# Rope attention and a squared-ramp MLP on one core: the same steps issued in another order, and some copies on the other engine

## The chip, the cores and the metric

The kernel runs on one core of a Trainium2 chip. The metric is device time in microseconds (us) of one execution; a kernel's time is the median of several executions. Engines are named as the profile names them: PE (TensorE matmul), PEld (its weight loads), DVE (VectorE), ACT (ScalarE), POOL (GpSimd) and SP (SyncE, which here issues every DMA).

## What is computed

Four batches, eight heads, 576 tokens, head size 64; then an MLP over the 2304 tokens (512 to 2048 to 512). The reference, cut to what matters:

```python
q_rot, k_rot = (rotate(q), rotate(k))              # rotary positions, halves x1, x2
scores = scale * np.matmul(q_rot, k_rot.transpose(0, 1, 3, 2))
scores = scores - np.max(scores, axis=-1, keepdims=True)
attn = np.exp(scores)
attn = attn / (np.sum(attn, axis=-1, keepdims=True) + 1e-09)
x = heads_together(np.matmul(attn, v))              # 2304 x 512
h = x @ w_in
g = np.where(h >= 1, h, np.where(h <= -1, 0.0, (h + 1) ** 2 / 4))
return g @ w_out
```

## The kernel before

**Precision.** Most operands are held as two f16 parts, a high part and a rest, and a product is three f16 matmuls (high by high, high by rest, rest by high). Splitting a tensor `x` with a factor `f` is one copy `high = f16(x*f)` and one `rest = x*f - high`. The copy may run on ACT (L311, L707) or on DVE (L313, L710). The ramp of the MLP has a square that runs on DVE (L696, one instruction) or on ACT (L698 and L699, two). The function `pick` reads the string `ON_VECTOR`, one digit per such choice in the order in which the plan is built: 1 is DVE, 0 is ACT.

**Stages.** Batch 0 works in f32: k and q are rotated on DVE by two products with the tables (L284, L285), summed on PE with an identity matrix (L302, L303, two matmuls into a PSUM region `psX`) and copied out by ACT (L306), or summed on DVE (L292). A score group (L555 for batch 0, L557 later) fills two PSUM tiles, `psS0` and `psS1`, one per head, columns 0 to 575; `psX` is the columns from 576 on of the same two tiles. Softmax of a group, `softmax_item`: DVE takes each head's maximum (L527), ACT the exponential with its sum (L529, L532), DVE a reciprocal (L534), then each head's high copy and rest (L538). A DMA transpose (L240) turns the result into `pT`, and PE multiplies by v (L605); `x_out` (L616, L619) writes x. An MLP block of 256 tokens is 8 steps: L684 into `psH`, ACT's ramp L701, the square, L704, the high copy, L712, then L721 into `psO`; at the end ACT copies out (L732) and SP stores.

**Weights.** The 16 weight chunks (8 of w_in, 8 of w_out, 1 MB each) come as 64-bit numbers (L236). DVE packs each in three instructions (L486, L488, L490), ACT makes the high copy (L311), PE forms the rest (L423, L424), ACT writes it (L427). Of the first chunk of each matrix a scale is measured first: two squares on ACT (L245), a sum over partitions on PE (L252), five or six tiny DVE instructions (L257, L259, L262, L269, L502). v's scale is measured the same way: three squares of `rv` and `rvL` (L245) and one L252.

**What sets the order.** `Plan.add` collects 2140 steps, each for one engine, with the tiles that it reads and writes. Nothing is scheduled at run time: `Plan.order` walks the table `ORDER`, each number being the place of the next step in the list of those still left, and the steps are issued in that one sequence. Each engine then works through its own steps in that order, and the waits between engines follow from which step stands first in the whole sequence. Two steps that touch the same PSUM bank wait for each other even if their columns differ, the later one in the sequence for the earlier one. The number `F32_SCORES` is a cost noted with batch 0's score steps; the issued sequence does not read it.

Of the kernel before, what the change touches and what calls it, by code (L numbers as in the profile page):

```python
# [21 lines left out]


ORDER = """
# [54 lines left out]
"""  # L79


PE_TILES = 16
PE_SUMS = 4
PE_V = 1
F32_SCORES = 1060.0
ON_VECTOR = (
    "00000000000000000000000000000000000000000000000000000000000000000000011100001000000000000000000000100100"
    "10101000011001010000110101000001101101000100000110000111000110100001011101000000010001111101101111010110"
    "10100110100010110000011000101000011001000011001001110111100001011111110010110101011001010010100111000101"
    "1000011001111111"  # L90
)


class Plan:


    def __init__(self):
        self.steps = []
        self.writer = {}
        self.readers = {}  # L100
        self.group = "init"
        self.part = ""
        self.free = []
# [36 lines left out]
def kernel(  # L140
# [187 lines left out]
    def qFkeys(hf, j):  # L328
        return [("qT", hf, 2 * (j % 2) + e, j // 2) for e in range(2)]
# [213 lines left out]
    def scores(at, b, t, j):  # L543
# [16 lines left out]
        if b == 0:  # L560
            plan.add("pe", F32_SCORES, at, mm, r=qFkeys(hf, j) + [("kT", ks, j, x) for x in range(2)],
                     w=[("psS", 0), ("psS", 1)], mode="rows")
# [312 lines left out]
```

## Time and profile before

| | before |
|---|---|
| median of 3 runs | 636.51 us (634.36 to 637.54) |
| the profiled execution's own time | 638.57 us |
| its span, first to last instruction | 636.8 us |
| PE busy | 591.4 us (93%) |
| DVE busy | 510.9 us (80%) |
| ACT busy | 417.3 us (66%) |
| mean granted TensorE clock | 0.96 |

Busy time is the time in which an engine has an instruction under way. The share is an average over the span: what an engine's idle time costs is read in the stretch where it falls. [...] The profiled execution is one run, 2.1 us above the median of the three.

### The profile page before, as it was taken

How to read it: one execution, taken by the hardware profiler on the slowest of the kernel's cores; microseconds unless marked ns; L12 is line 12 of the kernel's file. 1: busy time of each engine (PE TensorE's matmuls, PEld its weight loads, DVE VectorE, ACT ScalarE, POOL GpSimd, SP SyncE). 2: the span in 40 equal slices, each digit the busy share in tenths (PEclk: the TensorE clock that was granted, in tenths of full speed). 3: DMA queues.
4: the chain of work that ended last, by engine and by line, in shares of the span. 5: the costliest groups of instructions: out<-in, count | busy, mean ns of one | idle time of the engine just before them, and what ended most of it. 6: DMA issues, size and time to landing. Idle time of an engine off the chain costs nothing.

```text
span 636.8 us, 12019 instructions
## 1 busy us (share of the span) xinstructions
PE 591.4 (93%) x4770; PEld 379.4 (60%) x4770; DVE 510.9 (80%) x823; ACT 417.3 (66%) x843; POOL 0.7 (0%) x6
## 2 busy tenths in 40 slices
PE   4668878998999999999999999999999999999997
PEld 3343434655566667565666676666666666667674
DVE  5777597998999999999988999898989778854333
ACT  1666686988998878668787566655855765624321
POOL 0000000000000000000000000000000000000000
PEclk9775599999999999999999999999999999999999
DMA  8768799867485966677776643555764654550000
GB/s 308 275 200 205 228 219 294 211 168 180 123 217 143 220 137 137 153 165 151 146 157 154 159 108 66 98 90 104 131 125 91 127 95 97 79 87 34 1 34 18
DMA packets 182568, 91.29 MB, mean 143 GB/s; under 512 B 170608, under 2 KB 171888, under 8 KB 180464
## 3 DMA queue, kind: packets, MB, share of 16 engines
q1 hardware_dynamic: 182512, 90.52, 61.2%
q8 instruction: 37, 0.61, 0.4%
q14 instruction: 19, 0.16, 0.1%
HBM read 40.96 MB, written 4.72 MB: 72 GB/s over the span
## 4 chain that ended last, share of the span: by engine, by line
PE 52%; DVE 16%; ACT 7%; DMA 6%; issue 2%; SPq 0%; ACTq 0%; DVEq 0%
PE psH L684 20%; PE psO L721 20%; PE psV L605 4%; PE psS L557 4%; DMA pT<-phl 4%; DVE sca L527 3%; DVE phl L538 3%; ACT p L529 2%; PE psS L423 2%; DVE r L704 2%; DVE g L712 1%; DVE phl L313 1%; ACT phl L311 1%; PE psS L555 1%; DMA dup<-in_km_dram 1%
## 5 line engine op out<-in xcount | busy, mean ns | idle before, releaser
L684 PE MATMUL psH<-xT,w 128*128 128x256 f16 (+1 forms) x1920 | 205.1, 262 | 0.9 <-ACT a L701 0.9
L721 PE MATMUL psO<-w,g 128*128 128x512 f16 x864 | 201.4, 379 | 1.4 <-ACT o L732 0.8
L684 PEld LDWEIGHTS <-w 128*128 128x128 f16 x1920 | 170.5, 98 | 34.5 <-issue 3.2
L529 ACT ACTIVATE p<-psS,sca 128x576 f32<-128x576 f32 x144 | 105.6, 736 | 72.0 <-DVE sca L527 45.8
L721 PEld LDWEIGHTS <-g 128*128 128x128 f16 x864 | 82.0, 98 | 87.7 <-issue 3.5
L527 DVE TENSOR_REDUCE sca<-psS 128x1 f32<-128x576 f32 x144 | 106.0, 751 | 20.4 <-ACT w L427 4.7
L538 DVE SCALAR_TENSOR_TENSOR phl<-p,sca,phl 128x576 f16<-128x576 f32 x144 | 116.1, 812 | 6.9 <-ACT phl L311 6.2
L311 ACT ACTIVATE phl<-p,sca 128x576 f16<-128x576 f32 x98 | 73.8, 767 | 23.5 <-DVE sca L534 16.9
L701 ACT ACTIVATE a<-psH 128x512 f32<-128x512 f32 x72 | 42.5, 591 | 43.4 <-PE psH L684 35.4
L704 DVE SCALAR_TENSOR_TENSOR r<-a,r 128x512 f32<-128x512 f32 x72 | 49.4, 686 | 22.1 <-ACT r L699 21.4
L712 DVE SCALAR_TENSOR_TENSOR g<-r,g 128x512 f16<-128x512 f32 x72 | 49.5, 687 | 11.4 <-ACT g L707 9.3
L557 PE MATMUL psS<-kT,qT 64*128 64x64 f16 (+1 forms) x576 | 44.8, 284 | 2.6 <-ACT p L529 2.6
L605 PE MATMUL psV<-pT,vS 128*64 128x256 f16 (+1 forms) x512 | 43.3, 293 | 0.4 <-DVE sca L262 0.4
L557 PEld LDWEIGHTS <-qT 64*128 64x128 f16 x576 | 22.7, 94 | 32.7 <-issue 16.2
L427 ACT ACTIVATE w<-psS,sca 128x341 f16<-128x341 f32 (+1 forms) x48 | 25.4, 539 | 17.0 <-PE psS L555 8.3
L707 ACT ACTIVATE g<-r 128x512 f16<-128x512 f32 x40 | 24.9, 623 | 17.0 <-DVE r L704 7.1
L698 ACT ACTIVATE r<-a 128x512 f32<-128x512 f32 x46 | 28.8, 625 | 6.8 <-DVE g L712 5.6
L605 PEld LDWEIGHTS <-vS 128*64 128x64 f16 x512 | 27.1, 111 | 8.2 <-issue 4.9
L555 PE MATMUL psS<-kT,qT 64*128 64x512 f32 (+1 forms) x128 | 26.8, 510 | 4.0 <-ACT p L529 3.5
L699 ACT ACTIVATE r<-r 128x512 f32<-128x512 f32 x46 | 29.0, 630 | 1.5
L423 PE MATMUL psS<-xT,kT 128*128 128x341 f32 (+1 forms) x48 | 22.5, 558 | 7.8 <-ACT w L427 5.2
L423 PE MATMUL psS<-o,kT 128*128 128x341 f32 (+1 forms) x48 | 22.7, 561 | 6.4 <-DVE sca L527 3.2
(95 smaller groups left out, 539.6 us busy)
## 6 DMA issues: line engine op xcount, KB each, us to landing
w<-in_w_in_dram SPq DMA_DIRECT2D x7, 1024.0 KB, 5.5
w<-in_w_out_dram SPq DMA_DIRECT2D x6, 1024.0 KB, 6.7
rv<-in_vm_dram SPq DMA_DIRECT2D x8, 512.0 KB, 4.6
out_dram<-o SPq DMA_DIRECT2D x16, 256.0 KB, 2.4
rk<-in_km_dram SPq DMA_DIRECT2D x6, 576.0 KB, 5.1
dup<-in_km_dram SPq DMA_DIRECT2D x6, 576.0 KB, 4.6
dup<-in_qb_dram SPq DMA_DIRECT2D x4, 640.0 KB, 4.8
rq<-in_qb_dram SPq DMA_DIRECT2D x4, 640.0 KB, 6.2
```

Of the source, the lines that this page charges most:

```text
L311: plan.add("act", act_cost(n), at, lambda: nc.scalar.activation(out=hi, in_=x, func=AF.Copy, scale=f), r=r, w=w)
L423: nc.tensor.matmul(out=bank, lhsT=idn, rhs=y[:, cut], start=True, stop=False)
L527: plan.add("dve", dve_cost(S, psum=True), at, lambda m=m, src=src: nc.vector.tensor_reduce(out=m, in_=src, op=ALU.max, axis=AX.X, negate=T ...
L529: plan.add("act", act_cost(S, psum=True, ptrs=2), at, lambda a=a, e=e, m=m, src=src: nc.scalar.activation(out=p32[e], in_=src, func=AF.Exp ...
L538: plan.add("dve", dve_cost(S, ptrs=1), at, lambda a=a, e=e, hi=hi, lo=lo: nc.vector.scalar_tensor_tensor(out=lo, in0=p32[e], scalar=rr[:, ...
L557: nc.tensor.matmul(out=psS[a][:, lo:hi], lhsT=qT[hf][d, l, j, c:c + 128], rhs=kT[ks][d, j, m, lo:hi], start=z == 0, stop=z == 2)
L605: nc.tensor.matmul(out=outs[a], lhsT=st, rhs=moving(a, blk), start=z == 0, stop=z == len(seq) - 1)
L684: nc.tensor.matmul(out=psH[:, n * i:n * i + n], lhsT=wi[ft // 2][:, wl, kk, 128 * (ft % 2):128 * (ft % 2) + 128], rhs=xfn(xl, kk), start=z ...
L701: plan.add("act", act_cost(512, psum=True, ptrs=0), at, lambda one=one: nc.scalar.activation(out=a, in_=psH, func=AF.Relu, scale=2.0 ** -7 ...
L704: plan.add("dve", dve_cost(512), at, lambda one=one: nc.vector.scalar_tensor_tensor(out=r, in0=a, scalar=one, in1=r, op0=ALU.max, op1=ALU. ...
L712: plan.add("dve", dve_cost(512), at, lambda g=g, one=one: nc.vector.scalar_tensor_tensor(out=g[:, 1], in0=r, scalar=-one, in1=g[:, 0], op0 ...
L721: nc.tensor.matmul(out=psO[pos[tt]], lhsT=g[:, gl, n * i + 128 * tt:n * i + 128 * tt + 128], rhs=wo[ft // 2][:, wl, ft % 2, :], start=ft = ...
```

## The change

The table `ORDER` and the string `ON_VECTOR` are replaced, and `F32_SCORES` is another number. The steps are the same 2140, with the same tiles, and every buffer is the same. Of 328 choices 97 name DVE where 110 did: of the high copies more go from DVE to ACT than the other way, of the MLP's squares 19 go to DVE and 16 to ACT. Almost every step stays within some ten places of where it was on its engine.

```diff
 ORDER = """
-2 1 0 0 6 6 24 10 10 0 35 42 0 15 4 0 30 3 61 17 1 10 0 3 30 3 1 73 0 9 27 0 13 19 246 242 5 25 17 2 243 241 0
+3 1 0 0 49 13 6 19 6 1 22 28 0 8 0 38 13 14 23 3 7 25 1 56 15 0 12 1 31 3 70 15 1 0 28 5 22 25 22 0 235 11 238 14
...
-F32_SCORES = 1060.0
+F32_SCORES = 1132.0
...
-    "1000011001111111"
+    "1110100011000000"
```

**Place one, DVE's first ten rows after its constants.** The products with the rotary tables; `w` holds the second, rolled copy of k and q for batch 0, `rk` and `rq_85` the first. Before:

```order
L284 TENSOR_TENSOR rk<-rk,rt 128x576
L284 TENSOR_TENSOR w<-w,rt 128x576
L284 TENSOR_TENSOR rq_85<-rq_85,rt 128x256
L284 TENSOR_TENSOR w<-w,rt 128x256
L284 TENSOR_TENSOR rk<-rk,rt 128x576 x2
L284 TENSOR_TENSOR w<-w,rt 128x576
L284 TENSOR_TENSOR w<-w,rt 128x256
L284 TENSOR_TENSOR w<-w,rt 128x576
L284 TENSOR_TENSOR w<-w,rt 128x256
L284 TENSOR_TENSOR rk<-rk,rt 128x576
L527 TENSOR_REDUCE sca<-psS_93 128x1
```

Now:

```order
L284 TENSOR_TENSOR w<-w,rt 128x576
L284 TENSOR_TENSOR rk<-rk,rt 128x576
L284 TENSOR_TENSOR w<-w,rt 128x256
L284 TENSOR_TENSOR rq_85<-rq_85,rt 128x256
L284 TENSOR_TENSOR w<-w,rt 128x576 x2
L284 TENSOR_TENSOR w<-w,rt 128x256
L284 TENSOR_TENSOR rk<-rk,rt 128x576
L284 TENSOR_TENSOR rq_85<-rq_85,rt 128x256 x3
L284 TENSOR_TENSOR w<-w,rt 128x256 x2
L284 TENSOR_TENSOR rk<-rk,rt 128x576
L527 TENSOR_REDUCE sca<-psS_93 128x1
```

The last product that the first score group needs, the `w` 128x256 of the first head pair, was DVE's fourth instruction and is the seventh; the first maximum (L527) stands behind 14 products where it stood behind 11. SP's loads moved with them: the load for that product was the fifth and is the eighth, behind three more (128x256, 128x576, 128x256), and the load for the second of the two `w` 128x576 in front of it is the ninth.

**Place two, DVE and PE around the third score group** (L555; its two maxima are the two L527 here). `dup_88` and `rq_86` are the rest of batch 0's q, `o` the packed second weight chunk. DVE before:

```order
L534 RECIPROCAL sca<-sca 128x2
L527 TENSOR_REDUCE sca<-psS_93 128x1
L538 SCALAR_TENSOR_TENSOR phl_72<-p_1_70,sca,phl_72 128x576
L284 TENSOR_TENSOR rq_85<-rq_85,rt 128x256
L538 SCALAR_TENSOR_TENSOR phl_73<-p_2_71,sca,phl_73 128x576
L486 TENSOR_SCALAR o<-w 128x1024
L284 TENSOR_TENSOR w<-w,rt 128x256
L488 SCALAR_TENSOR_TENSOR o<-w,o 128x1024
L284 TENSOR_TENSOR rq_85<-rq_85,rt 128x256
L527 TENSOR_REDUCE sca<-psS_92 128x1
```

DVE now:

```order
L534 RECIPROCAL sca<-sca 128x2
L285 SCALAR_TENSOR_TENSOR dup_88<-dup_88,rt 128x1280
L527 TENSOR_REDUCE sca<-psS_93 128x1
L527 TENSOR_REDUCE sca<-psS_92 128x1
L538 SCALAR_TENSOR_TENSOR phl_73<-p_2_71,sca,phl_73 128x576
L490 SCALAR_TENSOR_TENSOR o<-w,o 128x1024
L538 SCALAR_TENSOR_TENSOR phl_73<-p_0_69,sca,phl_73 128x576
```

PE before:

```order
L555 MATMUL psS_92<-kT_62,qT_64 128x64
L555 MATMUL psS_93<-kT_62,qT_64 128x64
L302 MATMUL psS_93<-rk,kT_63 128x288
L303 MATMUL psS_93<-w,kT_63 128x288
L302 MATMUL psS_93<-rk,kT_63 128x288
L303 MATMUL psS_93<-w,kT_63 128x288
L302 MATMUL psS_92<-rq_85,kT_63 128x256
L303 MATMUL psS_92<-w,kT_63 128x256
```

PE now:

```order
L555 MATMUL psS_92<-kT_62,qT_64 128x64
L555 MATMUL psS_93<-kT_62,qT_64 128x64
L302 MATMUL psS_92<-rq_85,kT_63 128x256
L303 MATMUL psS_92<-w,kT_63 128x256
L302 MATMUL psS_93<-rk,kT_63 128x288
L303 MATMUL psS_93<-w,kT_63 128x288
```

The two maxima stand next to each other, where seven instructions stood between them; the sum of the third q pair stands in the whole sequence ahead of the maximum of `psS_92`, where it stood behind it. The second rest of `phl_73`, which the second DMA transpose waits for, was DVE's 50th step and is its 36th.

**Place three, ACT from the first high copies to the first weight squares.** `dup_87<-rv` are the squares of v. Before:

```order
L311 ACTIVATE phl_72<-p_0_69,sca 128x576
L306 ACTIVATE kT_62<-psS_93 128x288
L311 ACTIVATE phl_72<-p_1_70,sca 128x576
L306 ACTIVATE kT_62<-psS_92 128x288
L529 ACTIVATE p_2_71,sca<-psS_92,sca 128x576
L306 ACTIVATE qT_64<-psS_93 128x256
L529 ACTIVATE p_0_69,sca<-psS_93,sca 128x576
L532 ACTIVATE sca<-sca 128x2
L245 ACTIVATE r,sca<-xT_77 128x512 x2
```

Now:

```order
L311 ACTIVATE phl_72<-p_0_69,sca 128x576
L245 ACTIVATE dup_87,sca<-rv 128x1024 x2
L306 ACTIVATE qT_64<-psS_93 128x256
L529 ACTIVATE p_2_71,sca<-psS_92,sca 128x576
L306 ACTIVATE kT_62<-psS_92 128x288
L306 ACTIVATE kT_62<-psS_93 128x288
L529 ACTIVATE p_0_69,sca<-psS_93,sca 128x576
L532 ACTIVATE sca<-sca 128x2
L245 ACTIVATE r,sca<-xT_77 128x512
```

The two squares of v, each waiting for its half of `rv`, stand ahead of the copy of the second q pair and of the second group's exponentials; they stood some ten instructions behind.

## Rows read from the trace of the kernel before

**Rows 1.** Windows: us, then PE, PEld, DVE, ACT, POOL busy, PEclk, DMA share, GB/s

```profile
0.00:60.00 60.00, 37.71 (x113) 21.77 (x113) 39.48 (x75) 31.38 (x65) 0.70 (x6) 0.78 0.77 251
60.00:120.00 60.00, 50.56 (x290) 27.74 (x290) 48.54 (x66) 42.74 (x84) 0.00 (x0) 0.82 0.91 237
120.00:180.00 60.00, 56.49 (x356) 33.63 (x358) 53.06 (x77) 54.24 (x108) 0.00 (x0) 1.00 0.63 161
240.00:300.00 60.00, 57.77 (x527) 37.71 (x526) 56.86 (x92) 46.70 (x96) 0.00 (x0) 1.00 0.71 148
540.00:600.00 60.00, 60.00 (x454) 40.01 (x453) 32.26 (x54) 25.98 (x50) 0.00 (x0) 1.00 0.30 54
```

**Rows 2.** Timeline to the first maxima: start, us, engine, line, what [idle before <-releaser]

```profile
9.13 0.43 DVE L284 TENSOR_TENSOR w<-w,rt 128x256 f32<-128x256 f32 x1 [0.67 <-DMA w<-in_qa_dram]
...
11.21 1.30 PE L555 MATMUL psS<-kT,qT 64*128 64x512 f32 x8 [0.47 <-ACT qT L306]
...
12.60 1.43 DVE L284 TENSOR_TENSOR w<-w,rt 128x256 f32<-128x256 f32 x3 [0.35 <-DMA w<-in_qa_dram]
...
14.61 1.42 DVE L527 TENSOR_REDUCE sca<-psS 128x1 f32<-128x576 f32 x2
```

**Rows 3.** Timeline, third score group to the weight scale's sum

```profile
25.38 1.85 PE L555 MATMUL psS<-kT,qT 64*128 64x512 f32 x8
...
28.44 0.76 DVE L527 TENSOR_REDUCE sca<-psS 128x1 f32<-128x576 f32 x1 [2.92 <-PE psS L303]
...
31.81 1.05 ACT L245 ACTIVATE dup<-rv 128x1024 f32<-128x1024 f32 x1
...
33.31 0.75 DVE L527 TENSOR_REDUCE sca<-psS 128x1 f32<-128x576 f32 x1
...
34.12 1.22 PE L302 MATMUL psS<-rq,kT 128*128 128x256 f32 x2 [3.19 <-DVE sca L527]
...
39.61 0.43 PE L252 MATMUL psS<-sca 128*128 128x3 f32 x2
...
42.05 0.23 DVE L257 TENSOR_REDUCE sca<-psS 128x1 f32<-128x3 f32 x2 [4.19 <-PE psS L555]
```

**Rows 4.** Timeline, the second DMA transpose and what it waits for

```profile
46.57 0.81 DVE L538 SCALAR_TENSOR_TENSOR phl<-p,sca,phl 128x576 f16<-128x576 f32 x1
...
47.45 2.70 SPq L240 DMA_TRANSPOSE pT<-phl  x1
```

**Rows 5.** Windows, narrow ones, columns as in rows 1

```profile
42.00:44.00 2.00, 0.84 (x2) 0.30 (x2) 1.95 (x9) 0.78 (x1) 0.00 (x0) 1.00 0.04 11
44.00:46.00 2.00, 0.30 (x1) 0.10 (x1) 1.81 (x5) 1.34 (x2) 0.00 (x0) 1.00 0.01 4
60.00:80.00 20.00, 17.35 (x63) 8.52 (x63) 12.44 (x17) 10.79 (x22) 0.00 (x0) 0.56 0.81 215
```

**Rows 6.** Groups by line: xcount | busy us, mean ns of one | idle before

```profile
L311 ACT ACTIVATE phl<-p,sca 128x576 f16<-128x576 f32 x98 | 73.8, 767 | 23.5 <-DVE sca L534 16.9 <-DMA pT<-phl 2.9 <-DVE r L704 1.5
L699 ACT ACTIVATE r<-r 128x512 f32<-128x512 f32 x46 | 29.0, 630 | 1.5
L698 ACT ACTIVATE r<-a 128x512 f32<-128x512 f32 x46 | 28.8, 625 | 6.8 <-DVE g L712 5.6 <-DVE sca L534 0.7
L707 ACT ACTIVATE g<-r 128x512 f16<-128x512 f32 x40 | 24.9, 623 | 17.0 <-DVE r L704 7.1 <-PE psO L721 5.1 <-PE psH L684 4.4
L313 DVE TENSOR_SCALAR phl<-p,sca 128x576 f16<-128x576 f32 x46 | 23.7, 516 | 2.8 <-DMA pT<-phl 2.3
L696 DVE SCALAR_TENSOR_TENSOR r<-a 128x512 f32<-128x512 f32 x26 | 17.8, 685 | 12.6 <-ACT a L701 12.2
L710 DVE TENSOR_SCALAR g<-r 128x512 f16<-128x512 f32 x32 | 13.6, 424 | 4.7 <-PE psO L721 3.2
```

**Rows 7.** Timeline, the end

```profile
625.43 6.64 PE L721 MATMUL psO<-w,g 128*128 128x512 f16 x30
...
628.36 0.69 DVE L712 SCALAR_TENSOR_TENSOR g<-r,g 128x512 f16<-128x512 f32 x1
```

More of the change, by code (lines that the diff above doesn't have):

```diff
@@ L84 @@
 PE_V = 1
-F32_SCORES = 1060.0
+F32_SCORES = 1132.0
 ON_VECTOR = (
-    "00000000000000000000000000000000000000000000000000000000000000000000011100001000000000000000000000100100"
-    "10101000011001010000110101000001101101000100000110000111000110100001011101000000010001111101101111010110"
-    "10100110100010110000011000101000011001000011001001110111100001011111110010110101011001010010100111000101"
-    "1000011001111111"
+    "00000000000000000000000000000000000000000000010000010000000000000000000000010000000000000010000000000000"
+    "01100000001001100011010000000011010000010000100001100011001010001000110001011010101011010000011011000100"
+    "00001101100111010001001100100111011100100010110111011001001111101000101000000001110100011011011010110011"
+    "1110100011000000"
 )
```

106 rows, old and new, of the table ORDER are left out of this document.

## The prediction

> **What bounds the kernel now.** I read first the windows of 60 us. PE stands idle 22.3 us of the first 60, 9.4 of the next 60, 3.5 from 120 to 180, 2.2 from 240 to 300 and none from 540 on [rows 1]; its whole idle time is 45.4 us (636.8 less 591.4), so 31.7 of it, 70%, falls before 120 us. [...] The reader is to see two kernels in one: a start in which PE, DVE, ACT and DMA wait for each other in turn, and then a long stretch in which PE is full. PE's work is the same in both kernels, step by step. A new order can gain only where PE waits, so I read the start closely, in the timeline.
>
> From 120 to 300 us three engines are nearly full together (DVE 53.1 and 56.9 of 60, ACT 54.2 and 46.7) [rows 1]. A lead won in the start is therefore kept there if the work behind it is the same, and little is won anew.
>
> **The change part by part.** Working against the profiled execution (span 636.8, own time 638.57, which is 2.1 above the median of 636.51).
>
> *The start becomes later.* The last product for the first score group ran at 9.13, as soon as its load, the fifth, had landed; at 12.60 DVE waited for the tenth load [rows 2]. Between them five loads of 1,280 KB landed in 3.47 us: 369 KB/us. Now that product's load is the eighth, 544 KB later, so it lands at 9.13 + 1.5 = 10.6. On DVE it stands behind a 128x576 product whose load, 288 KB more, lands at 11.4; that one takes about 0.75 (the size of one maximum, L527 [rows 3]), the product itself 0.43 [rows 2], so it ends at 12.6 where it ended at 9.56. The first scores start 1.65 after it [rows 2]: 14.25 for 11.21, 3.0 later. DVE then has seven products left (five of 0.45, two of 0.75, together 3.7) ahead of the first maximum, which so starts at 16.3 for 14.61: part of the delay is already paid back, because before these products stood later.
>
> *The third scores.* They started at 25.38 [rows 3]. Now ACT has v's two squares in front, and the second waits for the twenty-first load. Up to it 6,816 KB are fetched, 5,408 more than at 9.13, which at 369 KB/us is 14.7 us: 23.8. A square takes 1.05 [rows 3], and then five instructions (three copies, two exponentials) of 0.4 to 0.75 come before the third scores, about 2.7 us: 27.6, or 2.2 later. PE's sums stand between them; a score group there took 1.85 where another took 1.30 [rows 2, 3], so up to 1.8 more can come from the slow clock. Bounds +2.2 and +4.0, taken in the middle: **+3.1**.
>
> *From the third scores to the weight scale's sum* (L555 at 25.38 to L252 at 39.61, 14.2 us [rows 3]). DVE took the first maximum at 28.44 and the second only at 33.31, since seven instructions stood between, and the sum of the third q pair, which needs its PSUM bank, waited 3.19 us for it [rows 3]. Now the two maxima are neighbours: the second follows 0.76 after the first instead of 4.87, 4.1 sooner, and the q sum stands ahead of it in the sequence and waits for neither. At least the 3.2 of PE's wait goes; if it and the 4.1 counted in series, 7.3. They overlap in part, so I take the middle: **-5.3**. What is late next is ACT, which has the two weight squares, v's third and the exponentials there in a row.
>
> The q sum writes columns from 576 on and the maximum reads those up to 575, and still it waited [rows 3]. [...]
>
> *The scale's first reduction.* L257 ran at 42.05, 2.0 after its matmul at 39.61 had ended, released by a score group (L555) that stood between in the sequence [rows 3]. Now L257 stands ahead of that group. The group takes 1.30 [rows 2]: **-1.3**; the bounds are 0 and 2.0.
>
> So the weight scale, on which all sixteen chunks hang, is ready some 3.5 us earlier.
>
> *SP.* The second transpose was issued at 47.45, when the second rest (46.57, 0.81 long) was done [rows 4]. SP stood before it, and the DMA engines were idle from 42 to 46 (share 0.04 and 0.01 [rows 5]). That rest moves up 14 places on DVE, ahead of the scale's tiny instructions, so the transpose and the loads behind it start some 8 us sooner; a load of k (576 KB) that stood at the fifty-first place is pulled ahead into that time as well. It is worth nothing if the loads were not late, and at most the 4 us of idle DMA; 60 to 120 is the stretch with DMA share 0.91 [rows 1], so something: **-0.8**.
>
> *Choices of engine.* 71 go from DVE to ACT and 58 back. A softmax high copy takes 0.767 on ACT and 0.516 on DVE, one of the MLP 0.623 and 0.424, a square 1.26 in two on ACT and 0.685 on DVE [rows 6]. Net, DVE loses 13 instructions, some 6 us; up to 300 us, where DVE is fullest, 17 go to ACT and 9 come, about 4 us. Hidden by PE after 300 us, so nothing there; before it, between -4 (all on the path) and +2 (ACT, 54.2 of 60 in one window, is late instead). It is nearest to the hidden case, since PE idles only some 8 us in that stretch: **-0.7**.
>
> *The end.* In the last step square and high copy both go to ACT: 1.26 - 0.685 + 0.623 - 0.424, so 0.77 longer. The last rest ended at 629.05; the last twelve of 30 matmuls, at 0.22 each, began at 629.3 [rows 7]. The new order puts one more group of three (0.65) in front. The cover is 0.25 + 0.65 = 0.9: nothing, and 0.77 at most if it is gone. All other moves are of a few places within full stretches: 0. The new `F32_SCORES` is read by no instruction: 0.
>
> Sum: 3.1 - 5.3 - 1.3 - 0.8 - 0.7 = **-5.0**, so 633.6 for the profiled execution and **631.5** beside the median.
>
> **The rivals.**
>
> *The late start is not made up (slower).* For it: 3 us at the first scores are certain by the loads, and ACT stands behind v's squares, waiting for a load that was no one's limit before. If the sums behind the third scores then wait for ACT instead of for the maximum, the gain of 5.3 is not there and the larger lag of 4.0 stays: 636.5 + 4.0 = 640.5. It decides where the weight scale's sum (L252) starts later than 39.61. Against it: PE's longest wait in that part named DVE [rows 3], and its cause is gone from the order.
>
> *The lead is lost before the MLP (no change).* From 60 to 120 us the DMA share is 0.91 [rows 1]. If the loads set when the first MLP step starts, a lead at 42 us ends there: 636, with what the choices of engine give, 635.5. Against it: the same loads start earlier too.
>
> [...]
>
> That the order does not act as it says is no rival of its own: only a table sets it.
>
> **How the numbers follow.** My forecast, 631.5, has 0.42 (its own range 628.5 to 633.3), the clock 0.12, the lost lead 0.28, the late start 0.18. 0.5%, about what a measurement of this kernel can tell from no change, is 3.2 us: faster means below 633.3, slower above 639.7. So faster 0.54, same 0.28, slower 0.18. The range takes in the clock's 626.5 with 2 us for its unknown size and reaches to the late start's 640.5: 624.5 to 640.5.
>
> **What would show it.** First scores near 14.3 and third scores near 28.5 in the timeline; then the two maxima of that group back to back, the wait of L302 for L527 gone, and L252 near 37.5, L257 right behind it. The second transpose should be issued before 40, and the DMA share from 42 to 46 should not be near 0. PE's first MLP step should start 3 to 5 us earlier, with the idle time of PE from 120 on as before. If L252 starts after 39.6, the forecast is wrong at the third scores; if it starts early and the first MLP step doesn't, it is wrong in DMA; if PE's idle time from 120 to 300 has grown, the choices of engine are to blame.

## The result, and the profile after

| | before | after |
|---|---|---|
| median, runs of the two beside each other | 636.18 us (634.36 to 637.54, 4 runs) | 617.05 us (613.99 to 618.41, 4 runs) |
| the profiled execution's own time | 638.57 us | 617.46 us |
| its span | 636.8 us | 615.7 us |
| PE busy | 591.4 us | 579.5 us |
| DVE busy, ACT busy | 510.9, 417.3 us | 507.0, 422.9 us |
| mean granted TensorE clock | 0.96 | 0.98 |

The ratio is 0.969 (95% interval 0.965 to 0.974): 19.1 us faster. The forecast was 631.5, the range 624.5 to 640.5. The direction was right; the gain is almost four times the forecast, and the time lies below the range.

The granted clock is the profile's, as a share of TensorE's full clock. In the kernel before it is 1.00 from 27 to 33 us, for one, and 0.50 from 48 to 77; "full" and "low" or "half" below stand for readings like these two.

The windows of 60 us after, as in [rows 1] (us, then PE, PEld, DVE, ACT and POOL busy, granted clock, DMA share, GB/s):

```profile
0.00:60.00 60.00, 40.41 (x133) 23.74 (x135) 45.68 (x83) 35.14 (x76) 0.71 (x6) 0.86 0.96 292
60.00:120.00 60.00, 52.59 (x363) 32.08 (x360) 56.51 (x75) 51.58 (x103) 0.00 (x0) 0.97 1.04 249
120.00:180.00 60.00, 60.00 (x449) 36.75 (x448) 59.66 (x92) 57.57 (x114) 0.00 (x0) 1.00 0.76 183
180.00:240.00 60.00, 59.34 (x552) 39.55 (x550) 57.71 (x91) 55.09 (x113) 0.00 (x0) 1.00 0.84 177
240.00:300.00 60.00, 59.79 (x529) 38.51 (x528) 56.87 (x92) 43.47 (x90) 0.00 (x0) 1.00 0.63 139
300.00:360.00 60.00, 57.09 (x555) 39.67 (x553) 50.96 (x86) 40.49 (x80) 0.00 (x0) 0.97 0.59 128
540.00:600.00 60.00, 60.00 (x499) 41.35 (x498) 22.33 (x34) 19.29 (x33) 0.00 (x0) 1.00 0.09 25
```

From 60 to 120 the clock is 0.97 where it was 0.82, and DVE does 56.5 us of work where it did 48.5 [rows 1]. From 120 to 180 PE stands still no more: 60.00, where it was 56.49 [rows 1]. One stretch is worse than before, 300 to 360: PE is busy for 57.09 us, where it was for 59.70 in the same window of before.

Where the 21 us between the two profiled executions arise is read from the start of the same step in both timelines:

| step | before | after | lead |
|---|---|---|---|
| first scores (L555) | 11.21 | 13.78 | -2.6 |
| third scores (L555) | 25.38 | 28.55 | -3.2 |
| weight scale's sum (L252) | 39.61 | 40.43 | -0.8 |
| its first reduction (L257) | 42.05 | 40.75 | +1.3 |
| fifth score group (L555) | 50.54 | 47.55 | +3.0 |
| first MLP step (L684) | 111.16 | 96.51 | +14.7 |
| second MLP block (L684) | 195.51 | 175.53 | +20.0 |
| span | 636.8 | 615.7 | +21.1 |

(The expectation of e6 below counts that score group, at 50.5 us before, as the fourth.) At 48 us the lead is 3.0, near the 3.5 that the forecast had for the weight scale. Then come 11.7 more before the first MLP step and 5.3 up to the second block. For all that the forecast had 0.8 (SP), 0.7 (choices of engine) and nothing for the other moves. Here is the stretch with most of it, 20 to 100 us, first before, then after (windows of 20 us, columns as above):

```profile
20.00:40.00 20.00, 14.43 (x38) 9.16 (x38) 14.86 (x19) 12.20 (x32) 0.00 (x0) 0.67 0.85 268
40.00:60.00 20.00, 13.50 (x40) 6.63 (x39) 13.78 (x33) 13.81 (x24) 0.00 (x0) 0.67 0.57 158
80.00:100.00 20.00, 15.03 (x75) 7.37 (x74) 18.08 (x25) 16.38 (x30) 0.00 (x0) 0.91 0.99 246
```

```profile
20.00:40.00 20.00, 16.30 (x38) 10.20 (x37) 14.63 (x17) 12.58 (x32) 0.00 (x0) 0.58 0.89 266
40.00:60.00 20.00, 13.37 (x63) 6.94 (x63) 19.16 (x40) 18.05 (x35) 0.00 (x0) 0.99 1.06 293
60.00:80.00 20.00, 14.95 (x99) 8.05 (x95) 17.99 (x25) 15.57 (x30) 0.00 (x0) 1.00 1.09 257
80.00:100.00 20.00, 17.64 (x134) 10.74 (x133) 18.87 (x26) 16.80 (x34) 0.00 (x0) 0.91 1.10 262
```

Three things go together from 40 to 80: the clock is 0.99 and 1.00 where it was 0.67 and 0.56 [rows 5], DVE and ACT work more (DVE 37.2 of the 40 us where it worked 26.2, ACT 33.6 where it worked 24.6), and the DMA share is 1.06 and 1.09 where it was 0.57 and 0.81. One trace can't tell which of them leads.

### The profile page after: what moved, and what is told of

It reads as the page before. It is cut to its first block, busy times and chain, and to the rows that moved or that the text cites. A ratio compares the mean times of both kernels' runs of the same rounds, so it can differ in the third digit from the quotient of the medians.

```text
span 615.7 us, 11999 instructions
## 1 busy us (share of the span) xinstructions
PE 579.5 (94%) x4770; PEld 375.3 (61%) x4770; DVE 507.0 (82%) x810; ACT 422.9 (69%) x853; POOL 0.7 (0%) x6
## 4 chain that ended last, share of the span: by engine, by line
PE 60%; DVE 19%; DMA 10%; ACT 7%; issue 4%; SPq 0%; DVEq 0%; ACTq 0%
PE psO L721 20%; PE psH L684 19%; PE psV L605 6%; DVE sca L527 4%; PE psS L557 4%; PE psS L423 3%; DVE phl L538 3%; DMA pT<-phl 3%; PE psS L555 2%; DMA vM<-vS 2%; ACT p L529 2%; DMA w<-in_w_out_dram 2%; DVE g L712 2%; DMA rk<-in_km_dram 2%; DVE r L704 2%
## 5 line engine op out<-in xcount | busy, mean ns | idle before, releaser
L684 PE MATMUL psH<-xT,w 128*128 128x256 f16 (+1 forms) x1920 | 204.9, 262 | 0.0
L684 PEld LDWEIGHTS <-w 128*128 128x128 f16 x1920 | 170.9, 98 | 34.1 <-issue 2.6
L529 ACT ACTIVATE p<-psS,sca 128x576 f32<-128x576 f32 x144 | 105.7, 737 | 56.4 <-DVE sca L527 42.1
L538 DVE SCALAR_TENSOR_TENSOR phl<-p,sca,phl 128x576 f16<-128x576 f32 x144 | 115.2, 812 | 3.8 <-ACT phl L311 3.2
L527 DVE TENSOR_REDUCE sca<-psS 128x1 f32<-128x576 f32 x144 | 106.2, 751 | 10.7 <-PE psS L557 6.9
L701 ACT ACTIVATE a<-psH 128x512 f32<-128x512 f32 x72 | 42.5, 590 | 52.0 <-PE psH L684 46.0
L605 PE MATMUL psV<-pT,vS 128*64 128x256 f16 (+1 forms) x512 | 43.5, 293 | 0.9 <-DMA pT<-phl 0.9
L557 PE MATMUL psS<-kT,qT 64*128 64x64 f16 (+1 forms) x576 | 43.8, 284 | 0.2
L707 ACT ACTIVATE g<-r 128x512 f16<-128x512 f32 x54 | 33.6, 623 | 13.9 <-DVE r L704 12.6
L557 PEld LDWEIGHTS <-qT 64*128 64x128 f16 x576 | 21.5, 94 | 29.5 <-issue 12.2
L696 DVE SCALAR_TENSOR_TENSOR r<-a 128x512 f32<-128x512 f32 x29 | 20.0, 688 | 20.9 <-ACT a L701 20.3
L605 PEld LDWEIGHTS <-vS 128*64 128x64 f16 x512 | 27.0, 112 | 9.5 <-issue 5.4
L698 ACT ACTIVATE r<-a 128x512 f32<-128x512 f32 x43 | 27.0, 627 | 8.0 <-DVE g L712 7.1
L605 PE MATMUL psV<-pT,vM 128*64 128x256 f16 (+1 forms) x320 | 26.2, 293 | 5.5 <-DMA vM<-vS 5.1
L529 ACT ACTIVATION_READ_ACCUMULATOR p<-psS,sca 128x1 f32 x144 | 28.3, 197 | 0.0
L699 ACT ACTIVATE r<-r 128x512 f32<-128x512 f32 x43 | 27.1, 630 | 1.4
```

Of the source, the lines that this page charges most:

```text
L527: plan.add("dve", dve_cost(S, psum=True), at, lambda m=m, src=src: nc.vector.tensor_reduce(out=m, in_=src, op=ALU.max, axis=AX.X, negate=T ...
L529: plan.add("act", act_cost(S, psum=True, ptrs=2), at, lambda a=a, e=e, m=m, src=src: nc.scalar.activation(out=p32[e], in_=src, func=AF.Exp ...
L538: plan.add("dve", dve_cost(S, ptrs=1), at, lambda a=a, e=e, hi=hi, lo=lo: nc.vector.scalar_tensor_tensor(out=lo, in0=p32[e], scalar=rr[:, ...
L557: nc.tensor.matmul(out=psS[a][:, lo:hi], lhsT=qT[hf][d, l, j, c:c + 128], rhs=kT[ks][d, j, m, lo:hi], start=z == 0, stop=z == 2)
L605: nc.tensor.matmul(out=outs[a], lhsT=st, rhs=moving(a, blk), start=z == 0, stop=z == len(seq) - 1)
L684: nc.tensor.matmul(out=psH[:, n * i:n * i + n], lhsT=wi[ft // 2][:, wl, kk, 128 * (ft % 2):128 * (ft % 2) + 128], rhs=xfn(xl, kk), start=z ...
```

## The experiments

**One change or two: the choices alone, the order alone.**

e1_choices, on the kernel before (the last line of the string; the others are replaced too):

```diff
-    "1000011001111111"
+    "1110100011000000"
```


> The order of before, with the engine choices of the change alone. If the new choices are what keeps PE full from 120 to 240 us (theory of the choices), this gains some 9 us, to about 627. If the order does all of it (theory of the order), it stays within 3 us of 636.

e2_order, on the changed kernel (likewise):

```diff
-    "1110100011000000"
+    "1000011001111111"
```


> The order of the change, with the engine choices of before. Theory of the order: 617, within 3. Theory of the choices: PE idles again from 120 to 240 us, and the time is near 626.

Both theories fell. The choices alone gave 650.41 (ratio 1.020, 1.014 to 1.025), 12.9 slower than the 637.47 beside them; the order alone 636.52 (0.999, 0.997 to 1.001), no change; the two together 19 faster. With the order before, the new choices cost 13 us; with the new order they save 19. So what the choices are worth depends on the order.

Both mismatched kernels lose in the same place, behind the first 200 us. The choices alone start the first MLP step at 110.5 and the second block at 194.8, as before; the order alone starts them at 94.9 and 175.7, as the changed kernel. That fits the table of choices: laid over the changed kernel's trace, none of the 129 choices that differ belongs to an instruction that runs before 145 us, and only 9 to one before 200. The start is a matter of the order alone; behind it PE waits. From 200 to 545 us PE stands idle for 4.9 us in the kernel before and 4.4 in the changed one, but for 13.6 with the choices alone and 18.1 with the order alone. The first three rows of PE's waits from 200 us on, first of the choices alone (200 to 545), then of the order alone (200 to 560, its lines one higher) and of the changed kernel (200 to 545); the columns are what PE waited with, for whom, us in total, times, the longest:

```profile
PE psS L557 <- ACT p L529: 6.2, 10, 1.1
PE psH L684 <- ACT a L701: 2.6, 5, 0.8
PE psS L583 <- ACT p L529: 2.1, 2, 1.5
```

```profile
PE psS L558 <- ACT p L530: 6.4, 10, 1.5
PE psV L606 <- DMA vM<-vS: 2.6, 2, 2.2
PE psH L685 <- ACT a L702: 2.4, 6, 0.6
```

```profile
PE psV L605 <- DMA vM<-vS: 2.9, 2, 2.4
PE psV L605 <- DMA pT<-phl: 0.9, 2, 0.7
PE psV L605 <- DMA vM<-vM: 0.4, 1, 0.4
```

In the changed kernel no row of that stretch names ACT, and in the kernel before L557 waits for ACT 5 times, 2.6 us in all. With the choices of the other order ACT's exponentials (L529) and ramps (L701) come late, in pieces of about half a microsecond. Here is the longest of these waits in e1. ACT was itself idle and waited for the second maximum (L527), and ahead of that maximum DVE had a high copy (L313 at 416.42) that ran on ACT before:

```profile
416.42 0.51 DVE L313 TENSOR_SCALAR phl<-p,sca 128x576 f16<-128x576 f32 x1
417.57 0.75 DVE L527 TENSOR_REDUCE sca<-psS 128x1 f32<-128x576 f32 x1
418.36 0.74 ACT L529 ACTIVATE p<-psS,sca 128x576 f32<-128x576 f32 x1 [0.99 <-DVE sca L527]
419.24 0.93 PE L583 MATMUL psS<-kT,qT 64*64 64x512 f16 x23 [1.45 <-ACT p L529]
```

So a moved copy can stand in the way on DVE, and not only in ACT's own queue. How much of the loss comes from such copies, and from which, was not tried.

**Where the order gains: four pieces of it.** e3_start50 takes the change's order for its first 153 steps and the order before for the rest; e4_start100 does so for 333 steps, to the first MLP step; both keep the choices before. e5_rest and e6_rest50 are the complements: the kernel before for 338 or 147 steps, then the changed order, with the changed choices. As first and last lines of the tables, e3 (and e4, which differs further in) and e5 (e6 has the same end, its lines broken elsewhere) against the kernel before:

```diff
-2 1 0 0 6 6 24 10 10 0 35 42 0 15 4 0 30 3 61 17 1 10 0 3 30 3 1 73 0 9 27 0 13 19 246 242 5 25 17 2 243 241 0
+3 1 0 0 49 13 6 19 6 1 22 28 0 8 0 38 13 14 23 3 7 25 1 56 15 0 12 1 31 3 70 15 1 0 28 5 22 25 22 0 235 11 238
```

```diff
-0 5 0 4 0 3 0 2 0 1 0 0 0 0 0 0 1 0
+10 0 0 8 8 15 15 0 7 13 0 6 2 0 4 8 0 0 6 0 5 0 11 4 0 3 8 3 7 7 0 6 0 5 0 0 3 0 2 0 1 0 0 0 0 0 0 0 0
```

> The first 153 steps of the change's order (to the fifth score group, about 48 us), then all others in the order of before; choices of before. Theory of the early start: the lead of 3 us at 48 us grows by itself, since TensorE's clock is then full from 40 to 80 us and the loads come early: the first MLP step starts near 98 us and the time is 622 to 625. Rival, the order of 50 to 100 us does it: only the 3 us stay, 633.

> The first 333 steps of the change's order (to the first MLP step, 97 us), then the order of before; choices of before. Lead of 14.6 us at the first MLP step in any case. If the 120 to 240 us stretch gains only because the loads and the weights are early there, 616 to 618; if its own order gains the 7 us there, 622 to 624.

> The kernel before up to its first MLP step (338 steps, some 110 us), from there the changed order and the changed choices. Theory of separate parts: the changed start alone gave 14.4 us (623.1), the whole change 20; if the parts add, the later part alone gives the other 6: 630 to 632, with the start as before (first MLP step near 111) and PE's idle time from 120 to 240 less by some 6 us. Rival, the late part only pays behind the early start (its loads and buffers are ordered for a block that starts 14 us sooner): 636 to 638.

> The kernel before for the first 147 steps (to the fourth score group, 50.5 us), from there the changed order and choices. Theory that the order from 48 to 97 us gains by itself: only the lead of 3 us at 48 us is missing, so 617 + 3 = 620 to 622, and the first MLP step at 99 to 101. Rival, that the first 50 us prepare what is gained later (the loads that fly at 42 to 48, the clock that stays full from 40 on): the first MLP step at 106 to 111, and 628 to 632.

| kernel | L252 | fifth scores | first MLP step | second block | time | ratio (interval) |
|---|---|---|---|---|---|---|
| before | 39.6 | 50.5 | 111.2 | 195.5 | 637.47 and 637.65 beside them | |
| e3, first 50 us new | 35.2 | 42.4 | 102.2 | 186.9 | 630.52 | 0.989 (0.983 to 0.994) |
| e4, first 97 us new | 38.7 | 46.0 | 94.8 | 180.8 | 623.10 | 0.978 (0.974 to 0.983) |
| e6, all but the first 50 us new | 38.2 | 49.4 | 102.9 | 183.7 | 624.31 | 0.978 (0.973 to 0.983) |
| e5, new from the first MLP step on | 40.1 | 51.2 | 109.7 | 190.9 | 630.47 | 0.988 (0.984 to 0.991) |
| after | 40.4 | 47.6 | 96.5 | 175.5 | 617.05 | 0.969 (0.965 to 0.974) |

The parts add. The start alone gives 14.4 and the rest alone 7.2, together 21.6 for the measured 19.1, with 2 to 3 us of uncertainty on each. The first 50 us alone give 7.0, all but them 13.3, together 20.3. So for e5 the theory of separate parts held. For e6 both theories missed: it comes out between them. e3, too, lies between its two expectations; e4 is in the range of 622 to 624.

The first 50 us are worth 6 to 7, though they show a lead of only 3.0 at 48 us in the changed kernel. That is no lead which grows by itself: in e3, where the clock happened to be full from 20 to 44 us (0.97 to 1.00), the lead stands at 8.1 at the fifth scores and at 8.9 and 8.6 at the two MLP marks. The moves behind 50 us gain without the first ones: in e6 the lead is 1.1 at the fifth scores, 8.3 at the first MLP step and 11.8 at the second block.

The share of the rest (7 us, with matching choices) grows from the first MLP step to the third block: e5 leads the kernel before by 1.5 us at the first MLP step, 4.6 at the second block and 7.9 at the third (243.4 and 251.3). PE's waits of 112 to 300 in the kernel before:

```profile
PE psS L557 <- ACT p L529: 2.6, 5, 1.0
PE psS L423 <- ACT w L427: 2.3, 4, 0.7
PE psO L721 <- ACT o L732: 0.8, 1, 0.8
PE psS L423 <- ACT p L529: 0.8, 1, 0.8
PE psS L423 <- DVE sca L527: 0.7, 1, 0.7
PE psH L684 <- ACT a L701: 0.6, 3, 0.3
PE psO L721 <- DVE g L712: 0.6, 1, 0.6
```

They are sixteen waits of half a microsecond, 8.4 us in sum. In the changed kernel the same view of 97 to 300 has one row, L605 on a transpose, 0.9 us; in e5 the view of 112 to 300 sums to 3.5. Which of the many small moves removes them was not tried.

**The clock or DMA?** In the kernel before the clock is low from 47 on (0.50 from 48 to 77 us) and DMA stands still from 44 to 48 (share 0.00). e7_fill gives PE something to do in the first hole, e8_dma gives DMA something.

e7_fill, on the kernel before (`zero` is the part of `vZ` that is set to 0 at the start, 64 partitions of 512, so a filler matmul is 64x128 by 512 and not 128x128 as the expectation has it; no step of the kernel writes `psO[1]` before 117 us in its trace):

```diff
+    k = ring("rest", 1000)
+    fill = (10, 3) if k == 0 else (0, 2) if k < 9 else (0, 0)
...
     nc.tensor.matmul(out=bank, lhsT=idn, rhs=y[:, cut], start=True, stop=False)
+    for _ in range(fill[0]):
+        nc.tensor.matmul(out=psO[1], lhsT=zero[:, 0:128], rhs=zero, start=True, stop=True)
     nc.tensor.matmul(out=bank, lhsT=neg, rhs=hi[:, cut], start=False, stop=True)
+    for _ in range(fill[1]):
+        nc.tensor.matmul(out=psO[1], lhsT=zero[:, 0:128], rhs=zero, start=True, stop=True)
```


> The kernel before, with short f16 matmuls of zeros (128x128 by 512, into a PSUM tile that nobody reads yet) in PE's idle time at the first weight chunk: ten between L423 and L424 of the first piece, three behind it, two behind each of the next eight pieces. They compute nothing. Theory of the clock: the half clock of 47.0 to 77.7 makes the f32 pairs of L423 take 1.3 to 1.5 us instead of 0.84 and lies on the path there; if the filler keeps the granted clock full there, the first MLP step comes 4 to 8 us sooner than at 110.5 and the time is 629 to 633. Rival, the clock only follows the idle time and nothing waits for it: the clock is full and the time is 636 to 638. If the clock falls in spite of the filler the run says nothing on the two.

e8_dma, on the kernel before, as rows of SP (on DVE the L538 that the transpose waits for moves ahead of two L527):

```diff
 L236 DMA rk<-in_km_dram 128x1152
+L236 DMA w<-in_w_in_dram 128x2048
 L240 DMA_TRANSPOSE pT_74<-phl_73 128x18x128
 L236 DMA dup_88<-in_km_dram 128x1152
-L236 DMA w<-in_w_in_dram 128x2048
```


> The order and choices before with four steps moved: the load of the third w_in chunk ahead of the second transpose instead of behind it, the L538 that the transpose waits for ahead of the two maxima of 44.24 and 45.90, the transpose and the next load behind it. Theory of DMA: the DMA engines stood still from 42 to 48 (share 0.41, then 0.00); filling that with a megabyte brings all later loads some 2 us forward, and the time is 633 to 635.5. Rival, DVE waited for no load between 46 and 80 us: 636.5 to 638.

e8 gave 638.37 (1.001, 0.998 to 1.003): the idle DMA of 44 to 48 is worth nothing. The gap only moved: the DMA share rises from 0.00 to 0.94 from 44 to 48 and falls from 0.82 to 0.36 from 48 to 60. e7 kept the clock full from 40 to 60 us (1.00), and in its profile the first MLP step starts at 105.5 instead of 111.2, and the second block at 191.0 instead of 195.5. The time, though, is 636.48 (0.998, 0.995 to 1.002), as the rival expected. The profiled executions differ by 2.7 us (635.85 and 638.57); the lead of 5.7 was partly lost behind 480 us, where PE was busy 57.71 of 60 us (59.95 before). So the clock delays the start, but e7 alone doesn't settle what that is worth at the end. The price of the low clock is seen in a pair of all but equal instructions in e7's trace, 0.84 us in the window from 52 to 60, where the clock is 1.00, and 1.51 in the one from 60 to 70, where it is 0.53 (start, duration, engine, line):

```profile
56.24 0.84 PE L426 MATMUL psS<-xT,kT 128*128 128x341 f32 x2 [0.20 <-ACT w L434]
...
60.74 1.51 PE L426 MATMUL psS<-xT,kT 128*128 128x342 f32 x2 [1.20 <-ACT w L434]
```

**The clock in the whole start.** e9_fill_after and e10_fill_before put the same filler into PE's idle times of the start, in the changed kernel (49 matmuls, to 41 us and around 80) and in the one before (113, to 98 us). e9, on the changed kernel; e10 has another table, and the filler of e7 with more pieces:

```diff
+FILL = {1: 12, 32: 2, 42: 4, 48: 1, 56: 3, 64: 9, 70: 2, 90: 2, 96: 2, 103: 1, 112: 1, 117: 1, 259: 2, 264: 2, 269: 5}
...
-        for fn in order:
+        for k, fn in enumerate(order):
             fn()
+            for _ in range(FILL.get(k, 0)):
+                nc.tensor.matmul(out=psO[1], lhsT=zero[:, 0:128], rhs=zero, start=True, stop=True)
```


> The changed kernel with short f16 matmuls of zeros in PE's idle times of the first 41 us (12 ahead of the first sum, 27 in the gaps from 13 to 41 us) and nine around 80 us; they compute nothing. In the changed kernel the granted clock is half from 23.3 to 40.4; in the run with the first 50 us of the change alone it happened to be full from 20 to 47, and the weight scale's sum came at 35.2 instead of 40.4. Theory, the start waits for PE at half clock: with the clock full the sum comes at 35 to 37, the first MLP step at 91 to 93 instead of 96.5, and the time is 612 to 614. Rival, from 40 us on DMA sets the pace (its share is above 1.0 from 40 to 80): the first MLP step stays at 95 to 97 and the time at 616 to 618.

> The kernel before with the same filler in PE's idle times from the start to 98 us (some 90 matmuls of zeros), so that the clock stays full where it was half (19.7 to 26.5, 33.4 to 40.2, 47.0 to 77.7, 94.8 to 98.2). The filler at 43 to 59 us alone brought the first MLP step from 111.2 to 105.5. Theory, the clock is most of what the change gained before the MLP: the first MLP step at 97 to 101 and, less what is given back later, 625 to 630. Rival, the order is most of it and the clock some 5 us: the first MLP step at 103 to 106, 632 to 636.

e10 gave 629.72 (0.988, 0.985 to 0.991): 7.7 faster, in the span that the theory of the clock set, though the first MLP step (103.7) lies in the rival's. Windows of e10 (PE's busy time now includes the filler) and the step's row:

```profile
20.00:40.00 20.00, 17.55 (x76) 9.14 (x75) 16.64 (x28) 14.06 (x36) 0.00 (x0) 1.00 0.89 291
40.00:60.00 20.00, 17.48 (x67) 6.86 (x65) 17.48 (x31) 15.28 (x27) 0.00 (x0) 1.00 0.85 165
60.00:80.00 20.00, 19.16 (x122) 10.10 (x122) 15.45 (x22) 14.83 (x29) 0.00 (x0) 1.00 1.06 257
```

```profile
103.74 1.48 PE L695 MATMUL psH<-xT,w 128*128 128x256 f16 x12
```

The clock is 1.00 where it was 0.67, 0.67 and 0.56, and DVE does 8.5 us more work from 20 to 80 us without any change in its order (49.57 us, where it did 41.08).

So in the kernel before the low clock of the start cost 7.4 us at the first MLP step. The executions without filler say the same of the end. The kernel before ran 13 times beside e1 to e4 and 19 times beside e5 to e8, with mean granted clocks of 0.959 to 0.979. The straight lines through the two sets have 3.0 and 2.5 us less for each 0.01 of clock. (In the 7 executions beside e9 to e12, which lie closer together, 0.961 to 0.972, it is 0.5.)

With filler the changed order starts the first MLP step at 94.9 (e9), 8.8 before e10, in one profile each:

```profile
94.90 1.36 PE L689 MATMUL psH<-xT,w 128*128 128x256 f16 x11
```

At the fifth scores that lead was 2.2 (43.83 and 46.03), so 6.6 of the 11.7 us between these two marks are the order's own. The other 5 are there only without filler. The clock is not what the change lives on, though: e9 and e10 ran beside each other, with a clock of 0.93 and 0.98 in the first 100 us (0.90 and 0.76 without filler), and e9 is still 19.4 us faster.

e9 gave 610.32 (0.956, 0.954 to 0.958), better than expected and some 7 us faster than the changed kernel (8 by the two ratios). By it L252 came at 36.7 instead of 40.4, but the first MLP step only 1.6 earlier (94.9), so up to there the rival was nearly right. The profiled executions differ by 4.3 (613.16 and 617.46); where the rest of the 7 arises is open.

**Can the later part be better still?** e11_splice takes the changed order and choices for 1122 steps (to 293 us) and those before for the rest; e12_splice_fill adds e9's filler. As the table's first lines and the last digits of the choices, against the kernel before:

```diff
-2 1 0 0 6 6 24 10 10 0 35 42 0 15 4 0 30 3 61 17 1 10 0 3 30 3 1 73 0 9 27 0 13 19 246 242 5 25 17 2 243 241 0
+3 1 0 0 49 13 6 19 6 1 22 28 0 8 0 38 13 14 23 3 7 25 1 56 15 0 12 1 31 3 70 15 1 0 28 5 22 25 22 0 235 11 238
...
     "1000011001111111"
```


> The changed order and choices for the first 1122 steps (to 293 us), then the order and choices before for the rest. Theory, order and choices are a matched pair and either pair does for the later part: PE loses 5.4 us in the part behind in the kernel before and 9.4 in the changed one (a stall at 317 to 334 of 5 us), so 612 to 614.5. Rival, a seam in the middle costs what a mismatch costs, as the order alone lost 18 us after 200: 620 to 630.

> The spliced kernel with the filler of the first 41 us. If both theories hold they add: 607 to 610. If the start's clock is given back: as the splice alone, 612 to 614.5. If the seam costs: 616 or more.

e11 gave 618.11 (0.970, 0.968 to 0.972), e12 615.18 (0.965, 0.962 to 0.969). Neither theory held: the seam costs nothing like a mismatch, but e11 is no faster than the changed kernel (0.969), and e12 is 4.9 us slower than e9, which differs from it only in the later part. So the later part of before is no better, seam included. The reason for the splice was a wait of the changed kernel at 326 to 331, where PE needs a part of v that is moved by DMA after DVE has split it, and DVE had stood for a load:

```profile
317.76 1.23 DVE L284 TENSOR_TENSOR dup<-dup,rt 128x1024 f32<-128x1024 f32 x1 [1.72 <-DMA dup<-in_qa_dram]
```

```profile
329.56 0.30 PE L605 MATMUL psV<-pT,vM 128*64 128x256 f16 x2 [2.37 <-DMA vM<-vS]
330.40 0.97 PE L605 MATMUL psV<-pT,vM 128*64 128x256 f16 x8 [0.54 <-DMA vM<-vS]
```

In e11 PE's waits of 290 to 330 have no such row, but one of 2.3 us for L732 at the seam. The fastest kernel of the study is therefore e9, the changed kernel with filler.

## Why the prediction was wrong, step by step

*The start becomes later* came out in number: first scores 14.25 forecast, 13.78 measured; first maximum 16.3 and 15.21. The first of these is in part luck. The last product did not wait for its load and ended at 11.48, not 12.6; the scores came 2.30 behind it instead of 1.65, since PE's last two sums in front of them took 1.06 and 0.99 where they took 0.59 each before.

*The third scores* were right, and by the named path: 28.5 forecast, 28.55 measured, behind v's second square, which waited for its load:

```profile
24.76 1.06 ACT L245 ACTIVATE dup<-rv 128x1024 f32<-128x1024 f32 x1 [1.95 <-DMA rv<-in_vm_dram]
```

*From the third scores to the weight scale's sum*, -5.3 forecast, -2.4 in the profile (11.88 instead of 14.23 us). The cause that was named is gone: the q sum (L302) runs at 32.17 without idle time, and the maxima start 2.01 apart instead of 4.87 [rows 3], though not 0.76, because the second waited 1.25 for the q sum, now ahead of it (in other columns of the same PSUM tile), as the sum had waited 3.19 for the maximum [rows 3]:

```profile
32.27 0.76 DVE L527 TENSOR_REDUCE sca<-psS 128x1 f32<-128x576 f32 x1 [0.66 <-PE psS L555]
34.28 0.76 DVE L527 TENSOR_REDUCE sca<-psS 128x1 f32<-128x576 f32 x1 [1.25 <-PE psS L303]
```

What came late next was PE, not ACT. From 24 to 40 us its clock was 0.50. In e3, with the same steps and a clock of 0.97 to 1.00 from 20 to 44, the same stretch took 8.04 us (27.18 to 35.22), but the 14.23 of before were not at full clock either (0.50 from 34 to 40). With filler in both it is 11.59 in the order before (e10, 24.05 to 35.64) and 8.30 in the new one (e9, 28.42 to 36.72): -3.3, at the lower bound of 3.2. The term was mis-sized; the middle of the bounds was too much.

*The scale's first reduction*, -1.3 forecast, -2.1 measured: L257 follows its matmul by 0.32 instead of 2.44. The bounds went to 2.0.

*SP*, -0.8 forecast. The second transpose was issued at 37.66, before 40 as said, and the DMA share from 42 to 46 is 0.93 and 1.03. But e8 showed that filling the gap alone is worth nothing, the lower bound.

*Choices of engine*, -0.7 forecast, with "Hidden by PE after 300 us, so nothing there". This step failed: it priced the choices apart from the order. The same 129 choices cost 12.9 us in one order and save 19.5 in the other (636.52 to 617.05), nearly all behind 200 us, where PE is nearly full and waits in pieces of half a microsecond.

*"All other moves are of a few places within full stretches: 0."* This is the step that cost most, a term put at nothing for a reason that the rows did not bear out: PE was busy 37.71 and 50.56 of 60 us before 120 us [rows 1]. Between 48 and 97 us the lead grows by 11.7. With filler in both kernels 6.6 of that are the order's own (e10 and e9), and e6, which has the new order only from 50 us on, gains 7.2 there. Behind it the moves give 7 more, with the choices that belong to them (e5). There PE's 8 us of idle time from 120 to 300 were counted, but "little is won anew" was concluded from three engines being nearly full.

*The end* came out as forecast, nothing, though the last twelve matmuls of before began at 629.41 (0.221 each), not 629.3.

*The clock*, 0.12 at 626.5. No run shows the 5 us by which that time lies below the forecast. What the runs showed: the low clock lay on the path, and with a granted clock of 1.00 from the start to 80 us the kernel before gains 7.7 (e10). As the reason for the change's gain the rival fell: with filler in both kernels the change is worth the same 19 us.

*The late start is not made up*, 0.18: its point of decision was L252 later than 39.61, and L252 did come at 40.43. The rival fell all the same, since L257 behind it came 1.3 earlier. The mark was put one step too early, and it hung on the clock of one execution: in e2, e3 and e4, which issue the same first 150 steps, L252 came at 38.6, 35.2 and 38.7.

*The lead is lost before the MLP*, 0.28: it fell. The DMA share is 1.04 from 60 to 120, higher than before [rows 1], and yet the lead grew from 3.0 to 14.7.

## What to carry to other kernels

Take an order of steps and a choice of engines for them as one variable: here, tested apart, each looked like nothing or worse. So cost the pair, and read where they mismatch by PE's idle time in many small pieces, most of it behind ACT. In a start in which several engines wait in turn don't set the many small moves at 0: a lead of 3 us grew to 15 here, where the wait of PE that the forecast took on was 3.2. Look at the granted clock in such a start too: short matmuls of zeros in PE's idle time (113 and 49) were worth 7.7 us in one order and some 7 in the other, beside the 19 of the change.

## What was not expected of the hardware

The clock in the first 50 us differs between executions of the same steps. The changed kernel, e2, e4 and e3 share their first 150 steps, with the same engines; L252 came at 40.4, 38.6, 38.7 and 35.2. Windows of 4 us of the changed kernel and of e3 (columns as above):

```profile
24.00:28.00 4.00, 3.58 (x8) 2.45 (x8) 4.00 (x5) 2.55 (x6) 0.00 (x0) 0.50 0.94 375
28.00:32.00 4.00, 4.00 (x10) 1.95 (x8) 2.51 (x4) 3.31 (x9) 0.00 (x0) 0.50 1.30 198
...
36.00:40.00 4.00, 3.50 (x9) 2.55 (x9) 3.03 (x3) 1.88 (x6) 0.00 (x0) 0.50 0.42 106
...
48.00:52.00 4.00, 2.12 (x12) 1.07 (x9) 3.98 (x9) 3.96 (x6) 0.00 (x0) 1.00 1.22 209
```

```profile
24.00:28.00 4.00, 3.22 (x10) 1.65 (x10) 4.00 (x5) 3.15 (x8) 0.00 (x0) 1.00 0.93 372
28.00:32.00 4.00, 3.64 (x15) 2.03 (x14) 4.00 (x7) 3.97 (x12) 0.00 (x0) 1.00 1.22 188
```

Here the records show PE fully busy at half clock (4.00 of 4 us at 0.50, changed kernel, 28 to 32), and busy for only 2.12 of 4 us at full clock (1.00, 48 to 52). So in this patchy start neither the busy share nor the order told the clock; only the granted clock of the run did, and a single profile of it carries an uncertainty of several microseconds in a step's time: 5.2 for L252 among the four above.
